# Retention attention and a SoLU MLP on one core: the whole run's written order planned anew, with q, k and v loaded by steps of their own

## The chip, the cores and the metric

The kernel runs on one core of one Trainium2 chip. The time is the device time in microseconds of one execution; lower is better. TensorE (PE), VectorE (DVE), ScalarE (ACT) and GpSimd (POOL) compute, and SyncE (SP) issues nearly all DMA transfers. All engines run their own instructions in order and wait for one another by semaphores.

## The reference

The inputs are q, k and v of 8 batches x 8 heads x 576 positions x 64, w_in (512x1024), w_out (1024x512) and g_ln (1024), all f32. The output is 4608x512 f32.

```python
# attention, for each batch and head
scores = q @ k.T / sqrt(64)
gamma  = 1 - 2.0 ** (-5 - head)
D[i,j] = gamma ** (i - j) if i >= j else 0
x      = (scores * D) @ v            # then heads side by side: 4608 x 512

# MLP
h    = x @ w_in
solu = h * softmax(h)
ln   = (solu - mean(solu)) / sqrt(var(solu) + 1e-6) * g_ln
out  = ln @ w_out
```

## The kernel before

**Tiles.** The 4608 tokens are cut into 36 chunks of 128. Nine chunks serve two batches: chunks 9g+0 to 9g+7 are four chunks of each of the two batches in turn, and chunk 9g+8 holds the last 64 tokens of both. The decay matrix is split into factors of the row and of the column, which go into q and v, and a triangular mask; what earlier chunks of a batch add comes through a running state of k times v, kept per batch.

**Steps of one chunk n**, with the names that the order uses:

- `ld` (L270, L274): loads q, k and v, three DMAs of 256 KB, on SyncE's queue.
- `cq` (L290, or L279), `ck` (L243), `cv` (L279): scale q, cast k, scale v, f32 to f16. A letter behind the chunk gives the engine: a is ACT, v is DVE, g is POOL.
- `tq` (L251): TensorE transposes of q and k into PSUM, and `eq` (L243) the copy to `qkT`. For late chunks k comes by a DMA transpose instead (`kd`, L326), and q by TensorE (`tr`, copied by `er`), or, for chunk 34, by a DMA as well (`kq`, L331).
- `sc` (L381): the scores; `mk` (L394, DVE): the mask.
- `kv` (L405), `ad` (L418, L420), `dk` (L432), `d3` (L444): this chunk's k times v, added to the state and scaled by the decay.
- `av` (L456) and `fs` (L256): scores times v, and q times the state; `ex` copies the sum to `xT`.
- `m1`, or `mr` a quarter at a time (h, L256): x times w_in into PSUM, 16 matmuls of 128x512.
- `mx` (L512), `xp` (L518), `so` (L527), `ce` (L538, L543, chunks 0 to 4 alone), `sq` (L553, L555), `ra` (L566 to L572), `rp` (L581): maximum, exponential, product, and the moments for the norm.
- `tu` and `eu`: TensorE transposes of u and the copy to `uT`; or `du` (L594): a DMA transpose of u on SyncE's queue.
- `m2` (o, L256): uT times w_out, 16 matmuls; `st` (L615, L621): scale rows on ACT, store on SyncE's queue.

The last chunk, 35, goes in halves (`hm` to `hw`). `li` and `wi` load and cast w_in in four pieces of rows; `lo` and `wo` (L789, L797) load w_out in four pieces and scale its rows by g_ln. `mm`, `mc` and `ws` (L821) take its column means away, for the chunks from 5 on. `wu` runs warm-up matmuls on zeros.

**Order.** One string, `ORDER`, lists all steps of the whole run. They are issued in just that order under a manual schedule, so each engine, and SyncE's queue too, has its steps in this order and stands still at a step whose data isn't there yet. `BANKS` gives the PSUM bank of each allocation, and `SLOTS` the slot in the SBUF ring of each tile, in the order in which they are allocated. A load waits on SyncE until its slot is free, and what stands behind it on that queue waits with it; a `du` or `kd` waits likewise for the u or k that it turns. h has two slots of two banks each.

Of the kernel before, what the change touches and what calls it, by code (L numbers as in the profile page):

```python
# [13 lines left out]
P = 128  # L14
# [15 lines left out]
tq:4 so:1 kv:4 ad:4 eq:4:a ce:1 sc:4 mk:4 cq:3:g ck:3:g tq:3 cv:3:g ld:5 xp:0 m1:2 eq:3:a so:0  # L30
kv:3 av:4 fs:4 cq:5:g lo:0 sq:1 tu:1 ex:4:a ck:5:g tq:5 eq:5:a ad:3 sc:3 ra:1:g dk:3 eu:1:a mx:2
xp:2 ce:0 m1:4 ld:6 mk:3 lo:3 mx:4 tu:0 eu:0:a sc:5 cv:5:g dk:1 cq:6:g ck:6:g wu:1:2 av:3 fs:3
xp:4 ex:3:a lo:2 kv:5 mk:5 av:5 wo:0:a fs:5 ex:5:a so:2 cv:6:g ce:2 d3:4 wo:1:g tq:6 kv:6 ad:6
lo:1 so:4 m1:3 d3:3 eq:6:a tu:2 wo:5:a ad:5 eu:2:a sc:6 wo:7:g m1:5 ld:8 rp:1 ce:4 wo:6:v mx:3
wo:3:a tu:4 eu:4:v wo:4:g wo:2:a m2:0 ld:7 sq:0 ra:0:g rp:0 m2:1 mk:6 mx:5 av:6 cq:7:v xp:3 so:3
sq:4 ra:4:v ld:9 mm:0 mc:0:v ws:6:v ws:4:v sq:2 ce:3 d3:5 ck:8:v dk:4 fs:6 ws:5:v st:1 ra:2:v
ck:7:g ws:0:v tq:7 st:0 m2:2 ex:6:a eq:7:a xp:5 cq:8:g tq:8 eq:8:a sc:7 rp:4 mk:7 m1:6 tu:3 ld:10
rp:2 st:2 ld:12 ld:11 ws:2:g sc:8 m2:4 sq:3 ws:1:v so:5 ld:13 eu:3:a dk:5 cv:7:v sq:5 mk:8 st:4
mx:6 av:7 ra:3:g rp:3 ws:7:v ck:9:a ck:10:v dk:6 fs:7 ex:7:a xp:6 m2:3 st:3 tu:5 cv:8:v kv:7 ad:7
cq:9:g so:6 tr:9 ws:3:v m1:7 dk:7 av:8 fs:8 ra:5:v rp:5 cq:10:g eu:5:a sq:6 ra:6:g er:9:va rp:6  # L40
ex:8:v mx:7 m2:5 st:5 sc:9 tu:6 eu:6:a mk:9 xp:7 so:7 ld:14 cv:9:g m1:8 av:9 kv:9 ex:9:a ck:12:a
ad:9 tr:10 mx:8 cq:12:g m2:6 cq:11:g tu:7 eu:7:v er:10:a sc:10 mk:10 ld:18 st:6 m1:9 cv:11:g sq:7
ra:7:v dk:9 cv:10:g kv:10 ad:10 ck:11:g dk:10 tr:11 xp:8 so:8 cq:13:g tr:12 av:10 rp:7 er:11:a
ex:10:a sq:8 er:12:v mx:9 m2:7 ld:15 tu:8 cq:18:g ld:17 sc:11 mk:11 eu:8:a ra:8:v cv:12:g xp:9
so:9 st:7 m1:10 rp:8 kv:11 ck:14:a av:11 d3:9 cv:13:g d3:10 fs:11 ex:11:a m2:8 ad:11 sc:12 mx:10
cq:14:g ck:13:a kv:12 ad:12 d3:12 m1:11 tu:9 ld:16 sq:9 ra:9:g st:8 tr:14 mk:12 mx:11 dk:11 xp:10
ld:19 er:14:v eu:9:a av:12 fs:12 so:10 cq:15:g cv:14:g ld:21 ex:12:a tr:13 er:13:a ck:15:a m2:9
ld:20 cq:17:v xp:11 sc:13 mk:13 tu:10 rp:9 st:9 so:11 m1:12 av:13 dk:12 fs:13 cq:16:v sc:14 mk:14
eu:10:a m2:10 sq:10 ex:13:a sq:11 kv:14 ad:14 ck:17:a mx:12 ra:11:v tu:11 cv:18:g eu:11:v cv:15:g
av:14 fs:14 ra:10:g rp:10 st:10 kv:13 m1:13 ex:14:a xp:12 d3:11 ad:13 tr:15 mx:13 so:12 du:12  # L50
ck:18:a er:15:a m2:11 xp:13 ld:22 sc:15 rp:11 st:11 dk:14 cv:16:g ck:16:g tr:16 d3:14 m1:14 d3:13
kv:15 ck:19:g mk:15 er:16:a sq:12 sc:16 av:15 dk:13 fs:15 ra:12:g so:13 ad:15 rp:12 mk:16 ex:15:a
mx:14 dk:15 cq:19:v tu:13 eu:13:a tr:17 er:17:av kv:16 xp:14 m1:15 av:16 fs:16 cq:21:g ad:16 dk:16
m2:13 sq:13 so:14 du:14 mx:15 ra:13:g rp:13 ex:16:a sc:17 mk:17 sq:14 st:13 m2:12 cv:22:v cv:17:g
av:17 fs:17 ld:23 ck:21:g tr:18 xp:15 ra:14:g so:15 ex:17:a er:18:av ld:24 m1:16 mx:16 sc:18 rp:14
ck:22:a st:12 sq:15 tu:15 mk:18 eu:15:a cq:22:g xp:16 ck:20:v ra:15:v rp:15 so:16 du:16 m2:14
tr:19 av:18 tr:21 ld:27 er:21:v st:14 m1:17 kv:18 ad:18 ex:18:a mx:17 cq:20:g tr:20 er:19:a sc:19
mk:19 er:20:a ld:25 cv:19:g m2:15 kv:19 ad:19 xp:17 cv:20:g so:17 d3:18 sq:16 ra:16:v cv:24:g
st:15 m1:18 dk:19 mx:18 av:19 sc:20 mk:20 ck:24:a rp:16 m2:16 ex:19:a cv:21:v dk:18 tu:17 kv:20
# [12 lines left out]
mk:28 st:20 m2:23 sq:24 ra:24:g tr:29 er:29:a av:27 m1:26 ra:23:v rp:23 ex:27:a rp:24 av:28 kd:31
mx:25 tr:30 xp:25 cq:31:g ex:28:a mx:26 ld:33 cv:30:g m2:22 so:25 du:25 st:23 sc:29 er:30:a mk:29
cq:32:g ck:32:g kd:32 tu:24 m1:27 xp:26 so:26 sc:30 mx:27 dk:27 st:22 kv:30 cv:31:g eu:24:a tr:32
ad:30 sq:25 d3:29 ra:25:g cv:32:g er:32:a dk:30 m1:28 kv:31 mk:30 ad:31 d3:31 xp:27 av:29 tr:31
# [4 lines left out]
so:29 du:29 m1:31 rp:27 cv:33:g kv:33 ad:33 st:27 mx:31 sq:30 m2:26 sc:34 cv:34:g mk:34 dk:33  # L80
dk:32 st:25 av:33 fs:33 xp:31 so:31 du:31 ra:28:v rp:28 ex:33:a m1:32 sq:29 av:34 kv:34 ad:34
fs:34 ex:34:a m1:33 mx:32 xp:32 m2:28 du:30 ck:35:g mx:33 xp:33 so:32 st:28 cq:35:g tr:35 er:35:v
ra:29:v rp:29 m2:29 ra:30:g so:33 sc:35 du:32 cv:35:g m1:34 du:33 mk:35 mx:34 sq:31 sq:33 dk:34
st:29 xp:34 ra:31:v rp:31 m2:31 st:31 rp:30 av:35 fs:35 rp:26 ex:35:v sq:32 so:34 du:34 m2:30
ra:32:g rp:32 ra:33:v hm:35:0 hx:35:0 st:26 st:30 hm:35:1 sq:34 hx:35:1 hp:35:0 m2:32 m2:33
ho:35:0 ht:35:0 hp:35:1 ho:35:1 hc:35 rp:33 ra:34:v ht:35:1 st:32 he:35:0:v hq:35:0:v rp:34 m2:34
he:35:1:v hq:35:1:a ra:35:v st:33 st:34 rp:35 h2:35:0 h2:35:1 hw:35:0:a hw:35:1:v
"""

BANKS = """  # L90
01231023102130121301320132013213022130232013120130212013201323013201320132013203103123001230213201
32012310231023103210320130123102130213012301032103202312030321321032103021321032113021320132132012
031132012302302102120201231232132321230123023
# [7 lines left out]
qf 012345601234561023456012345610235462  # L101
kf 012345012345021345012453012540312540
vf 012345601234561025346102350413620453
q16 012340123401234021032014321032410243
v16 012341023410234012431230124013240312
k16 012345120345120341520345124301523401
qkT 012301230123012302130210231021023103
ret0 012301230123012301230123012301230123
ret1 012301230123012301230123012301230123
t 01230120321032013201320321031210  # L110
xT 012301230123012301230123012301230210
# [754 lines left out]
```

## Time and profile before

| what | value |
|---|---|
| three runs | 211.17, 212.69, 213.72 us (median 212.69) |
| span of the profiled execution | 210.9 us; no other time of its own is recorded |
| TensorE clock | 1.00 in every stretch |
| DMA transposes | 16 of u, 7 of k, 1 of q |
| HBM read and written | 32.5 MB, 9.4 MB |

The span runs from the first to the last instruction of one execution, so it is a little less than the time of a run. Busy times are sums over the instructions of an engine. In a line that groups instructions, the figures behind the bar are the busy us, the mean ns of one, and the idle time just before them with what ended it. The DMA share is the mean over 16 DMA engines and can read a little over 1.

### The profile page before, as it was taken

To read this page: it belongs to the slowest core of one execution; us is meant where nothing else is said; L and a number is where in the kernel's file an instruction comes from. 1 tells how busy PE (TensorE), PEld (TensorE's weight loads), DVE (VectorE), ACT (ScalarE), POOL (GpSimd) and SP (SyncE) were. 2 spreads that over 40 slices of the span, in tenths; PEclk is the share of its full clock that TensorE was granted. 3 is DMA by queue.
4 is the path that set the end of the run, shared out by engine and by line. 5 is a ranking of instruction groups with operands and counts; after the bars stand their busy time and mean duration, and the time that the engine had idled before them with its cause. 6 is when DMAs were issued, how large, how long until landed. Compare 5 with 4: busy or idle time off the path is not lost.

```text
span 210.9 us, 7583 instructions
## 1 busy us (share of the span) xinstructions
PE 194.3 (92%) x3125; PEld 124.0 (59%) x3125; DVE 181.4 (86%) x323; ACT 170.5 (81%) x299; POOL 157.2 (75%) x226
## 2 busy tenths in 40 slices
PE   0887798999999999999999999999999998999992
PEld 0464476575666657657566667575656654565562
DVE  0486999979997999899989999999879998999760
ACT  2424999898979999999898978999679976677981
POOL 5377899676689899888839798879999977545620
PEclk9999999999999999999999999999999999999999
DMA  5999998999898989999999899999989999899754
GB/s 134 257 330 294 258 272 290 253 209 299 224 215 258 265 215 273 221 251 230 208 275 197 205 231 238 273 226 206 179 143 256 210 166 205 156 247 199 154 174 149
DMA packets 110834, 47.71 MB, mean 226 GB/s; under 512 B 94536, under 2 KB 104784, under 8 KB 110800
## 3 DMA queue, kind: packets, MB, share of 16 engines
q1 hardware_dynamic: 110480, 47.07, 99.7%
q8 instruction: 24, 0.39, 0.8%
q10 hardware_dynamic: 320, 0.16, 0.3%
q14 instruction: 10, 0.08, 0.2%
HBM read 32.54 MB, written 9.44 MB: 199 GB/s over the span
## 4 chain that ended last, share of the span: by engine, by line
PE 55%; SPq 14%; DMA 8%; DVE 8%; POOL 7%; ACT 3%; issue 3%; DVEq 0%; POOLq 0%
PE o L256 21%; PE h L256 18%; SPq L274 5%; SPq L270 5%; DMA w_out<-in_moe_w_out_dram 3%; PE tp L251 3%; PE sc L381 3%; PE lp L251 3%; DMA qkT<-k 2%; PE x L456 2%; POOL v L279 2%; SPq L789 2%; DMA qf<-in_q_dram 2%; PE x L256 2%; SPq L779 2%
## 5 line engine op out<-in xcount | busy, mean ns | idle before, releaser
L256 PE MATMUL h<-w_in,xT 128*64 128x512 f16 x560 | 66.9, 380 | 0.1
L256 PE MATMUL o<-w_c,uT 128*64 128x512 f16 x480 | 56.9, 380 | 0.0
L394 DVE TENSOR_TENSOR ret<-sc,tris 128x512 f16<-128x512 f32 x72 | 46.1, 682 | 2.8 <-PE sc L381 2.5
L256 PEld LDWEIGHTS <-xT 128*64 128x64 f16 x576 | 31.5, 110 | 23.1 <-issue 0.7
L512 DVE TENSOR_REDUCE nm<-h 128x1 f32<-128x1024 f32 x35 | 42.6, 1216 | 2.8 <-PE h L256 2.7
L256 PEld LDWEIGHTS <-uT 128*64 128x64 f16 x560 | 31.0, 110 | 23.0 <-issue 0.6
L527 DVE SCALAR_TENSOR_TENSOR u<-h,e 128x1024 f16<-128x1024 f32 x35 | 42.5, 1215 | 1.5 <-ACT e L518 1.4
L518 ACT ACTIVATE e<-h,nm 128x1024 f32<-128x1024 f32 x35 | 39.4, 1125 | 5.0 <-DVE nm L512 3.1
L432 POOL TENSOR_TENSOR s<-t,small 128x512 f16<-128x512 f32 x32 | 33.9, 1063 | 7.4 <-DVE t L420 6.1
L555 ACT ACTIVATE sq<-u,su 128x1024 bf16<-128x1024 f16 x30 | 34.8, 1159 | 2.0 <-DVE u L527 2.0
L581 POOL TENSOR_TENSOR rs<-w,mhalf 128x1 f32<-128x1 f32 x36 | 20.3, 570 | 20.7 <-DVE w L572 17.2
L290 POOL TENSOR_TENSOR q<-qf,small 128x512 f16<-128x512 f32 x30 | 31.2, 1043 | 5.4 <-DMA qf<-in_q_dram 5.1
L279 POOL TENSOR_TENSOR v<-vf,small 128x512 f16<-128x512 f32 x30 | 31.7, 1062 | 2.8 <-DMA vf<-in_v_dram 2.5
L615 ACT ACTIVATE o_sb<-o,rs 128x512 f32<-128x512 f32 x35 | 24.0, 692 | 4.5 <-POOL rs L581 3.2
L243 ACT COPY qkT<-tp 128x512 f16<-128x512 f16 x42 | 23.0, 599 | 5.0 <-PE tp L251 4.9
L243 ACT CAST xT<-x 128x512 f16<-128x512 f32 x29 | 17.1, 593 | 3.1 <-PE x L256 2.8
L251 PE MATMUL tp<-ident,q 128*64 128x128 f16 x232 | 12.4, 230 | 6.0 <-POOL q L290 5.5
L243 ACT CAST k<-kf 128x512 f16<-128x512 f32 x17 | 10.5, 626 | 7.7 <-DMA kf<-in_k_dram 7.7
L456 PE MATMUL x<-ret,v 128*64 128x128 f16 x288 | 14.8, 222 | 2.1 <-DVE ret L394 1.5
L251 PEld LDWEIGHTS <-q 128*64 128x64 f16 x280 | 11.0, 115 | 8.9 <-POOL q L290 5.7
L381 PE MATMUL sc<-qkT 64*128 64x128 f16 x288 | 14.7, 223 | 1.3 <-DMA qkT<-k 0.8
L444 POOL TENSOR_TENSOR s<-t,small 128x256 f32<-128x256 f32 x24 | 15.3, 638 | 0.9 <-DVE t L420 0.8
(87 smaller groups left out, 272.1 us busy)
## 6 DMA issues: line engine op xcount, KB each, us to landing
qf<-in_q_dram SPq DMA_DIRECT2D x36, 256.0 KB, 5.1
kf<-in_k_dram SPq DMA_DIRECT2D x36, 256.0 KB, 5.0
vf<-in_v_dram SPq DMA_DIRECT2D x36, 256.0 KB, 5.5
out_dram<-o_sb SPq DMA_DIRECT2D x35, 256.0 KB, 4.2
w_in<-in_moe_w_in_dram SPq DMA_DIRECT2D x4, 512.0 KB, 6.0
w_out<-in_moe_w_out_dram SPq DMA_DIRECT2D x4, 512.0 KB, 6.5
uT<-u SPq DMA_TRANSPOSE x16, 4.6
out_dram<-o_sbh SPq DMA_DIRECT2D x2, 64.0 KB, 1.8
```

The costliest lines, as they stand in the source:

```text
L243: (engine.copy if engine is nc.scalar else engine.tensor_copy)(out=out, in_=in_)
L251: nc.tensor.transpose(out=out[w], in_=in_[:, w], identity=ident)
L256: nc.tensor.matmul(out=out[w], lhsT=lhsT[:, w], rhs=rhs, start=start, stop=stop, skip_group_check=True,)
L279: engine.tensor_tensor(out=dst, in0=T.pop((key, n)), in1=table.unsqueeze(2).to_broadcast([P, H, D]), op=ALU.mult,)
L290: ENG[e].tensor_tensor(out=dst.rearrange("p (a h) d -> p h a d", h=2), in0=T.pop(("qf", n)).rearrange("p (h a) d -> p h a d", h=2), in1=ta ...
L394: nc.vector.tensor_tensor(out=r, in0=s, in1=m, op=ALU.mult)
L432: nc.gpsimd.tensor_tensor(out=s16, in0=t.unsqueeze(2).to_broadcast([P, 4, 2, D]), in1=gd.unsqueeze(3).to_broadcast([P, 4, 2, D]), op=ALU.mult,
L512: nc.vector.tensor_reduce(out=nm, in_=T["h", n], axis=AX.X, op=ALU.max, negate=True)
L518: nc.scalar.activation(out=e, in_=T["h", n], func=ACT.Exp, bias=T.pop(("nm", n)), accum_out=s)
L527: nc.vector.scalar_tensor_tensor(out=u, in0=T.pop(("h", n)), scalar=-1.0, in1=T.pop(("e", n)), op0=ALU.mult, op1=ALU.mult, accum_out=su,)
L555: nc.scalar.activation(out=s, in_=T.pop(("v", n)), func=ACT.Square, scale=-float(DFF), bias=T.pop(("su", n)), accum_out=ss,)
L615: nc.scalar.activation(out=o_sb, in_=T.pop(("o", n)), func=ACT.Copy, scale=T.pop(("rs", n)))
```

## The change

`ORDER`, `BANKS` and `SLOTS` are replaced as a whole. `ld` becomes three steps, `lq`, `lk` and `lv`, which issue the same DMAs and can be placed one by one; the first chunks' loads now have w_in's pieces between them. Which chunk uses `tq` and which `kd` with `tr` is said by the order alone. The number of rings and slots is as before.

```diff
-BY_DMA = 12
-BY_PE = (12, 13, 14, 15, 16, 18, 19, 20, 21, 22, 23, 24, 25, 27)
 ORDER = """
-c1:0 ld:1 ld:0 cq:1:g cv:1:v ck:1:a cq:0:g tq:1 eq:1:av wu:2:2 wu:5:2 ck:0:a cv:0:g sc:1 ld:2 mk:1
-tq:0 eq:0:av ck:2:a kv:0 ad:0 av:1 sc:0 mk:0 li:2 cq:2:g tq:2 ex:1:a li:3 eq:2:v dk:0 wi:3:1:a
...
-er:31:a ck:33:g so:27 du:27 fs:29 ex:29:a av:30 fs:30 ex:30:a ld:34 m2:24 tu:26 rp:25 mx:28 kd:33
-sc:31 eu:26:v sq:27 xp:28 cq:33:g mk:31 so:28 ra:27:v m1:30 mx:30 dk:31 tr:33 er:33:a st:24 m2:25
-dk:29 kv:32 sq:28 d3:30 ad:32 sc:32 m1:29 av:31 mk:32 xp:30 cq:34:g av:32 fs:32 ex:32:a so:30
-ck:34:g sq:26 fs:31 kd:34 kq:34 ex:31:v mx:29 du:28 m2:27 sc:33 ra:26:v ld:35 mk:33 d3:32 xp:29
...
+lv:1 lk:1 lv:0 lq:1 ck:1:v c1:0 cv:1:v cq:1:g li:0 cv:0:v lk:0 wu:2:4 tq:1 lq:2 kv:1 gt:0 ck:0:g
+wu:3:1 eq:1:av sc:1 wi:0:0:v mk:1 wu:6:4 kv:0 lq:0 cq:2:v li:3 c2:0 wi:3:1:v li:1 av:1 wu:8:3
...
+m1:30 du:27 lq:34 ra:25:g ad:31 ex:29:a dk:31 sc:31 so:28 ck:33:g st:24 mk:31 m2:25 sq:27 sq:26
+tr:33 d3:30 sc:32 d3:31 lq:35 mx:30 er:33:v m1:29 dk:30 kv:32 kd:33 mk:32 rp:25 xp:30 ra:26:g
+lv:33 rp:26 av:31 st:25 cv:33:g ad:32 fs:31 mx:29 m2:27 lk:35 sc:33 cq:34:g so:30 ex:31:a mk:33
+sq:28 av:32 xp:29 fs:32 kd:34 m1:31 sq:30 du:26 kq:34 so:29 av:33 ex:32:a du:29 fs:33 lv:34 kv:33
+ra:30:g du:28 mx:31 sq:29 xp:31 m1:32 cq:35:g lv:35 ex:33:v ck:35:v m2:26 ad:33 ra:27:g so:31
...
-    def ld(n):
-
-        for key, src in (("qf", q), ("kf", k), ("vf", v)):
-            dst = ring(load, [P, H, D], FP, key)
-            if key == "qf" and quads(n) or key == "kf" and chunks[n][1] == 4:
-                nc.sync.dma_start(
-                    out=dst.rearrange("p (h a) d -> p h (a d)", h=2), in_=fours(src, n)
-                )
-            else:
-                nc.sync.dma_start(out=dst, in_=tokens(src, n))
-            T[key, n] = dst
+    def load_one(n, key, src):
+        dst = ring(load, [P, H, D], FP, key)
+        if key == "qf" and quads(n) or key == "kf" and chunks[n][1] == 4:
+            nc.sync.dma_start(
+                out=dst.rearrange("p (h a) d -> p h (a d)", h=2), in_=fours(src, n)
+            )
+        else:
+            nc.sync.dma_start(out=dst, in_=tokens(src, n))
+        T[key, n] = dst
+
+    def lq(n):
+        load_one(n, "qf", q)
+
+    def lk(n):
+        load_one(n, "kf", k)
+
+    def lv(n):
+        load_one(n, "vf", v)
...
+    def both(n):
+
+        if ("qkT", n) not in T:
+            T["qkT", n] = ring(att, [P, 2, 4, P], F16, "qkT")
+        return T["qkT", n]
+
     def kd(n):
-        if chunks[n][1] == 4 or n < BY_DMA or n in BY_PE:
-            return
-        T["qkT", n] = ring(att, [P, 2, 4, P], F16, "qkT")
+
         nc.sync.dma_start_transpose(
-            out=T["qkT", n][:, 1], in_=T["k16", n].rearrange("p h d -> p (h d)")
+            out=both(n)[:, 1], in_=T["k16", n].rearrange("p h d -> p (h d)")
         )
...
     def tr(n):
-        if chunks[n][1] == 4 or n < BY_DMA or n in BY_PE:
-            return tq(n)
+
         tp = bank([P, 4, P], F16, "tr")
```

SyncE's queue, in the order written: before, the loads of chunk 1, 0 and 2, the four pieces of w_in, the loads of 4, 3 and 5, and then w_out's pieces around the loads of 6. After:

```
lv:1 lk:1 lv:0 lq:1 li:0 lk:0 lq:2 lq:0 li:3 li:1 lk:2 li:2 lv:2 lq:4 lk:4 lv:4 lk:3 lq:3 lv:3
lq:5 lk:5 lq:6 lv:5 lk:6 lo:2 lv:6 lo:1 lo:3 lo:0 lk:7 lq:7 lk:8 lq:8 lv:7 ...
```

Steps of each kind by engine, where the number changes (a is ACT, v DVE, g POOL):

| step | before | after |
|---|---|---|
| `cq` | g 31, v 5 | g 27, v 9 |
| `cv` | g 30, v 6 | g 28, v 8 |
| `ck` | a 17, g 15, v 4 | a 9, g 20, v 7 |
| `eu` | a 13, v 6 | a 15, v 3 |
| `ws` | g 1, v 7 | g 5, v 3 |
| `wi` | a 3, v 3, g 2 | a 2, v 3, g 3 |
| `ra` | g 19, v 17 | g 21, v 15 |
| `ex` | a 29, v 7 | a 30, v 6 |
| transposes of u: `du`, `tu` | 16, 19 | 17 (26 added), 18 |
| transposes of k by DMA: `kd` | 7 | 6 (29 left out) |
| warm-ups `wu`, pairs of matmuls | 10 | 15 |

More of the change, by code (lines that the diff above doesn't have):

```diff
@@ L30 @@
[L30 to L35, printed above, removed]
@@ new lines @@
+ws:1:g dk:6 lq:13 sc:7 so:5 mk:7 eq:8:a rp:4 lk:12 ws:5:g m1:6 kv:7 lk:11 lq:12 ws:7:v cq:9:v
+st:1 lq:14 cv:8:g lk:14 sc:8 ad:7 m2:4 ws:4:g lv:10 lk:13 tu:3 dk:7 lv:14 ck:9:a lv:13 mk:8 sq:5
+tu:5 lv:11 mx:6 eu:3:v sq:3 ra:5:g av:7 lk:21 st:4 xp:6 fs:7 ra:3:v tq:9 eq:9:va ex:7:a m2:3 sc:9
+cv:9:v so:6 rp:3 mk:9 m1:7 ws:3:v lv:12 eu:5:a kv:9 st:3 cq:11:g sq:6 ck:10:v ad:9 av:8 lv:15
+fs:8 rp:5 tu:6 mx:7 ck:11:g cq:10:g ra:6:g ex:8:a cv:10:g m2:5 lv:16 cq:12:g tq:10 rp:6 xp:7
+cq:14:g av:9 cq:13:v so:7 m1:8 lq:15 st:5 lk:16 ex:9:v tq:11 mx:8 eq:10:a sc:10 eu:6:a eq:11:a
@@ new lines @@
+du:14 dk:15 rp:13 rp:12 m2:13 ex:16:a lv:20 kv:18 ck:19:g xp:15 tq:17 cq:21:g m2:12 ad:18
+eq:17:va lk:25 sq:14 so:15 lk:24 dk:16 ra:14:v st:13 st:12 sc:17 sq:15 mk:17 m1:16 d3:18 sc:18
+av:17 mx:16 mk:18 xp:16 fs:17 rp:14 m2:14 ex:17:v tu:15 st:14 cq:19:g dk:18 tq:19 eu:15:a so:16
+av:18 kv:19 ra:15:v m1:17 eq:19:v tq:21 ad:19 ex:18:a ck:24:g rp:15 du:16 mx:17 lk:22 sq:16 lk:23
+sc:19 d3:19 cq:25:g mk:19 lv:22 m2:15 tq:20 xp:17 so:17 cv:20:g cq:23:g ra:16:g st:15 av:19
+eq:21:a dk:19 m1:18 cq:22:g kv:20 eq:20:v lv:21 lq:29 lv:24 ad:20 tu:17 ex:19:a mx:18 sc:20 sq:17
@@ new lines @@
+mx:33 d3:32 m2:29 av:34 so:32 fs:34 eq:35:a kv:34 st:27 ad:34 xp:33 ra:28:v ex:34:a m2:28 dk:33
+sq:32 so:33 sc:35 cv:35:g mk:35 m1:34 dk:34 du:31 st:29 rp:28 mx:34 av:35 fs:35 ra:32:g ex:35:v
+rp:30 m2:30 du:32 sq:33 ra:33:v xp:34 du:33 so:34 du:34 st:30 hm:35:0 hx:35:0 hm:35:1 rp:31
+hx:35:1 m2:31 st:28 m2:32 hp:35:1 rp:32 ho:35:1 hp:35:0 ho:35:0 ht:35:1 sq:34 m2:33 st:32 ht:35:0
+hc:35 hq:35:0:v hq:35:1:a he:35:1:v st:31 ra:34:v rp:33 rp:34 ra:35:g m2:34 rp:35 st:33 st:34
+he:35:0:v h2:35:0 hw:35:0:a h2:35:1 hw:35:1:v
@@ L88 @@
 """
 BANKS = """
[L91 to L93 removed]
+0123013013012301230231022310302130202130213201231230320132013102103213210321201320130210231023123013
+2033120123012230132032130213021032032103210321032031203103020213021031202301230203120231230123023012
+0320201320320132132132132023123120130102
@@ L100 @@
 SLOTS = """
[L101 to L107, printed above, removed]
+vf 012345601234560213650426135042613542
+kf 012345012345012340152403215432150342
+qf 012345601234560132460132460314250341
+k16 012345012435021435021430241502314250
+v16 012340123401234013240124302134213042
+q16 012340213042130241032013024032134021
+h 010101010101010101010101010101010101
+qkT 012301230123102310231023012301320312
 ret0 012301230123012301230123012301230123
 ret1 012301230123012301230123012301230123
-t 01230120321032013201320321031210
-xT 012301230123012301230123012301230210
-s16 01230132013201321032013021031201
-s32 012301230123013203120312
-h 010101010101010101010101010101010101
+t 01230123012301321023102313023103
+xT 012301230123012301230123012301230123
+s32 0123012031203102310231023
+s16 012302130213021302130213023013203
 e 01201201201201201201201201201201201
-u 01234013240132401324013241023412031
-uT 01234102341023410324102340123041230
+u 01234012340123401324013240123402103
+uT 01234210342130421034210341203412034
 o_sb 01230123012301230123012301230123012
@@ L331, in kq @@
         nc.sync.dma_start_transpose(
-            out=T["qkT", n][:, 0], in_=T.pop(("q16", n)).rearrange("p h d -> p (h d)")
+            out=both(n)[:, 0], in_=T.pop(("q16", n)).rearrange("p h d -> p (h d)")
         )
     def tr(n):
-        if chunks[n][1] == 4 or n < BY_DMA or n in BY_PE:
-            return tq(n)
         tp = bank([P, 4, P], F16, "tr")
@@ L344, in er @@
     def er(n, e="a"):
-        if chunks[n][1] == 4 or n < BY_DMA or n in BY_PE:
-            return eq(n, e)
-        turned(ENG[e], n, T["qkT", n][:, 0], T.pop(("tp", n)))
+        turned(ENG[e], n, both(n)[:, 0], T.pop(("tp", n)))
     def turned(engine, n, out, tp):
```

94 lines of the change are left out of this document (43 added, 51 removed).

## Prediction

> **What bounds the kernel now.** I read the share of each engine first, then the same shares in stretches of the run, then TensorE's waits in the long middle, and last the chain that ended last.
>
> ```profile
> span 210.9 us, 7583 instructions
> PE 194.3 (92%) x3125; PEld 124.0 (59%) x3125; DVE 181.4 (86%) x323; ACT 170.5 (81%) x299; POOL 157.2 (75%) x226
> PE 55%; SPq 14%; DMA 8%; DVE 8%; POOL 7%; ACT 3%; issue 3%; DVEq 0%; POOLq 0%
> ```
>
> TensorE is busy for 92% of the span and is more than half of the chain. VectorE follows at 86%. SyncE's queue and the transfers, 22% of the chain together, must lie somewhere in particular, which the stretches show (columns: stretch, its length, then busy us and count for PE, weight loads, DVE, ACT and POOL, then TensorE's clock, the DMA share and GB/s).
>
> ```profile
> 20.00:25.00 5.00, 3.48 (x60) 2.29 (x59) 4.24 (x7) 3.70 (x7) 4.36 (x6) 1.00 1.00 236
> 30.00:40.00 10.00, 9.32 (x175) 6.38 (x171) 9.79 (x18) 8.80 (x15) 9.61 (x12) 1.00 1.01 274
> 40.00:200.00 160.00, 157.20 (x2548) 99.51 (x2547) 148.44 (x257) 140.77 (x247) 125.54 (x176) 1.00 1.04 222
> 205.00:211.00 6.00, 2.08 (x36) 1.71 (x32) 0.66 (x2) 1.39 (x3) 0.55 (x1) 1.00 0.37 131
> ```
>
> There are three stages. Until 40 us the transfers are full and TensorE has gaps. From 40 to 200 us TensorE has 157.20 of 160 us, so 2.8 us are left to win there; DVE has 148.44, and the clock is full. The last 6 us are the tail of the last chunk, whose steps the change keeps. The chain says what the first stage waits for, and with what TensorE is filled later (start, us, what):
>
> ```profile
> 31.84 7.28 DMA w_out<-in_moe_w_out_dram
> 39.13 1.33 ACT w_out L797 x2
> ...
> 173.57 5.15 DMA qkT<-k
> ...
> 178.76 0.40 PE sc L381 x8
> ...
> 185.70 0.12 PE kp L405 x8
> 185.83 0.23 PE x L256 x8
> 186.05 1.73 PE h L256 x16
> 187.78 1.73 PE o L256 x16
> 189.51 0.45 PE tp L251 x16
> ```
>
> The first stage ends when the last piece of w_out has landed at 39.12 us and has been scaled at 40.46. Later the chain is matmul after matmul without a gap, except at 173.57, where the DMA transpose of k of chunk 33 holds the scores. TensorE's waits from 40 to 200 us (what waited, for what: total, times, longest):
>
> ```profile
> PE sc L381 <- DMA qkT<-k: 0.8, 1, 0.8
> PE x L456 <- POOL v L279: 0.5, 1, 0.5
> PE tp L251 <- DVE t L420: 0.5, 1, 0.5
> PE tp L251 <- DVE k L243: 0.4, 1, 0.4
> PE o L256 <- ACT w_out L797: 0.3, 1, 0.3
> PE tr L251 <- ACT o_sb L615: 0.3, 1, 0.3
> ```
>
> Six single waits make up the 2.8 us. No one of them recurs, so the written order before fits the chip almost everywhere.
>
> **The change, part by part.** No matmul for the result is added or removed. An h or o step costs the same 1.73 us at another place. u of chunk 26 leaves TensorE for a DMA transpose and k of chunk 29 comes to it, 0.45 and about 0.2 us, which I leave out as near zero. What can move the time is: the first 40 us, which engine does the small copies, and how much TensorE work stands between the issue of a transfer and its use.
>
> *The start.* The loads are now ordered one by one, and pieces of w_in go between them. But w_out's last piece stands in the SyncE queue behind 21 loads of 256 KB, four pieces of w_in and the three other pieces of w_out, before as after. With the DMA share at 1.00 to 1.01 the same bytes take the same time, and w_out lands at 39.1 us again. Ahead of the first step that needs w_out, TensorE has 23.8 us of written work before and 24.8 after, summed by the chain's prices; the difference is five more warm-ups of two 128x512 matmuls each, 5 x 2 x 1.73/16 = 1.1 us, and both sums lie well under 39 us. The warm-ups lie in gaps such as that between 20 and 25 us (3.48 busy of 5); without these they would cost 1.1. I take 0, from -0.3 (half of the 0.7 us in which TensorE is idle from 30 to 40 us) to +0.5 (half of the warm-ups).
>
> *Which engine copies.* By the written orders: q's scaling on DVE 5 to 9 (POOL 31 to 27), v's on DVE 6 to 8 (POOL 30 to 28), k's cast from ACT 17 to 9, on DVE 4 to 7, on POOL 15 to 20; uT's eviction on DVE 6 to 3, on ACT 13 to 15; centring of w_out on DVE 7 to 3, on POOL 1 to 5.
>
> ```profile
> L290 DVE TENSOR_TENSOR q<-qf,small 128x512 f16<-128x512 f32 x5 | 4.9, 982 | 1.1 <-DMA qf<-in_q_dram 1.1
> L290 POOL TENSOR_TENSOR q<-qf,small 128x512 f16<-128x512 f32 x30 | 31.2, 1043 | 5.4 <-DMA qf<-in_q_dram 5.1 <-POOL v L279 0.2
> L279 DVE TENSOR_TENSOR v<-vf,small 128x512 f16<-128x512 f32 x6 | 4.1, 690 | 6.1 <-DMA vf<-in_v_dram 6.1
> L279 POOL TENSOR_TENSOR v<-vf,small 128x512 f16<-128x512 f32 x30 | 31.7, 1062 | 2.8 <-DMA vf<-in_v_dram 2.5
> L243 ACT CAST k<-kf 128x512 f16<-128x512 f32 x17 | 10.5, 626 | 7.7 <-DMA kf<-in_k_dram 7.7
> L243 POOL CAST k<-kf 128x512 f16<-128x512 f32 x15 | 9.1, 609 | 0.9 <-DMA kf<-in_k_dram 0.7
> L243 DVE CAST k<-kf 128x512 f16<-128x512 f32 x4 | 1.8, 443 | 0.0
> L243 ACT COPY uT<-lp 128x1024 f16<-128x1024 f16 x13 | 13.3, 1022 | 0.5 <-PE lp L251 0.4
> L243 DVE COPY uT<-lp 128x1024 f16<-128x1024 f16 x6 | 4.1, 685 | 0.6 <-PE lp L251 0.5
> L821 DVE TENSOR_TENSOR w_c<-w_out,warm 128x512 f16<-128x512 f16 x7 | 3.4, 500 | 0.0
> L821 POOL TENSOR_TENSOR w_c<-w_out,warm 128x512 f16<-128x512 f16 x1 | 1.1, 1149 | 0.0
> ```
>
> DVE: 4 x 0.98 + 2 x 0.69 + 3 x 0.44 - 3 x 0.69 - 4 x 0.50 = +2.6 us. ACT: -8 x 0.63 + 2 x 1.02 = -3.0. POOL: -4 x 1.04 - 2 x 1.06 + 5 x 0.61 + 4 x 1.15 = +1.4. (Some smaller steps also change engine, one or two of a kind; they are left out.) DVE comes to 151 of 160 us in the middle stage, still under TensorE's 157.2, which covers it; without cover it would be +2.6. I take +0.3, since the nearer a second engine comes to the first the more often one waits for the other; bounds 0 to 2.6.
>
> *Waits of before.* A new order removes those 2.8 us where they were and may put as many elsewhere. It gives k of chunk 29 to TensorE instead of a DMA transpose, and ACT, at 140.77, 3.0 us of air. I take half, -1.4; bounds -2.8 to 0.
>
> TensorE's own figure may hide waits: in the trace its busy time counts modelled ends, and 157.20 is made of matmuls that overlap. The Trainium skill, "Perfetto Trace Analysis", section "Identifying the Most-Contended Engine", says that matmul busy time is not a good measure, since pipelined instructions look different from what they cost. By it more than 2.8 us may be there to win, and the term -1.4 would grow by half of what is hidden. The gapless chain at 185 us (0.12, 0.23, then 1.73 twice) bears the small figure out for that stretch only.
>
> *Transposes and loads at new places.* This is the largest part. Between the place where a transfer is written and its first use stands TensorE work, which I add up with the chain's prices (h or o 1.73 us, scores 0.3 to 0.4, x, fs and kv 0.1 to 0.2, transposes of a chunk 0.45). For the DMA transposes of u, from `du` to `m2`, this cover was 5.7 us at least before and 8.7 in the median; after, it is 2.4 for chunk 26, 3.3 for 23, 3.5 for 32, 4.1 for 31, 4.9 for 22, 5.0 for 27, 6.4 in the median. For k, from `kd` to `sc`, it was 8.9 for chunk 33 and 5.7 for 34; after, 2.2 for 33, 4.0 for 32, 5.1 for 30. The times from issue to landing, of uT and then of qkT:
>
> ```profile
> DMA to landing us min/median/max: 3.4/4.6/5.7
> ...
> DMA to landing us min/median/max: 2.5/3.1/5.1
> ```
>
> At the medians, issued just at their written place, they come late by 2.2 (26), 1.3 (23), 1.1 (32), 0.5 (31) and 0.9 (k of 33) = 6.0 us. At the longest it is 3.3 + 2.4 + 2.2 + 1.6 + 0.8 + 0.7 + 0.3 + 0.2 for u and 2.9 + 1.1 for k = 15.5. At best nothing: SyncE's queue goes in its own order and can be ahead of the written place (u of 26 is ready some 16 us of TensorE work before its `du`). It can also be behind: before, k of 33 was issued at 173.57, and its scores waited although 8.9 us of work stood between. What is late next is the o matmul or the scores, and behind them on TensorE everything, since it works in order. I take half of 6.0, +3.0; bounds 0 to 15.5.
>
> The loads' cover for v falls from 16.8 to 7.8 us in the median, for k and q it stays (10.0 to 9.4, 10.3 to 12.5).
>
> ```profile
> vf<-in_v_dram SPq DMA_DIRECT2D x36, 256.0 KB, 5.5
> ```
>
> Only v of chunk 33 is written with next to nothing, 0.2 us, before its scaling; that one holds POOL by 5.3 us, which has 34 of 160 us free, and 4.9 us more of TensorE work stand before `kv` needs it: 5.5 + 1.06 - 0.2 - 4.9 = 1.5 at full price. Queued behind it on POOL are q of 34 and a row scale. I take +0.4; bounds 0 to 1.5.
>
> **Sum.** 0 + 0.3 - 1.4 + 3.0 + 0.4 = +2.3. On the profile's span: 210.9 + 2.3 = 213.2. The runs' median lies 1.8 above the span, so 212.69 + 2.3 = 215.0.
>
> **Rivals.** *No change, 212.7:* the queue runs ahead wherever the cover is short, and the old waits come again at other places. For it speaks that the two u transposes with 5.7 us, the longest landing exactly, cost nothing before; against it that k of 33 was late with more.
> *Faster, 209.9:* transposes hidden as in the first rival, ACT's relief and the freely placed loads take away the waits of the middle stage, 212.69 - 2.8. It would decide if no transfer is waited for by TensorE. For it speaks that each q, k and v load can now stand where it is wanted, as POOL's 5.1 us of waits for q show; against it that TensorE's own waits from 40 us on hold none for a load, so that loads in better places have nothing of TensorE's to give back.
> *Late at full price, about 220:* SyncE's queue is held at its head by a slot or an unfinished u, as at 173.57, and all five late transposes cost in full: 212.69 + 6.0 + 0.3 + 0.4 to 1.5 = 219.4 to 220.5, with no old wait removed. It decides from the point where SyncE has no lead in the last third of the run.
>
> **How the numbers follow.** The forecast, transposes late at about half price, 213.5 to 217.5, has 0.40; no change 0.24; faster 0.26; full price 0.10. About 1%, 2.1 us, is what a measurement of this kernel can tell. Of the forecast a quarter, 0.10, lies under 214.8. So: faster 0.26, same 0.24 + 0.10 = 0.34, slower 0.30 + 0.10 = 0.40. The range goes from 209.5 (the faster rival with the best start, 212.69 - 2.8 - 0.3 = 209.6) to 219.5, which leaves out most of the full price and what might be won beyond the 2.8.
>
> **What would show it.** Right: in the changed profile TensorE waits in `o` for the transfer of uT and in `sc` for that of qkT, 2 to 4 us together, mostly after 130 us; the last piece of w_out lands at 39 to 39.5 us; TensorE's busy time is equal within 1.5 us, DVE's is up by some 2, ACT's down by 3. Wrong: w_out lands two us earlier or later (the start moves the time after all), or TensorE waits for no transfer in the middle stage (then the first two rivals), or it waits for POOL or DVE instead, which my sum puts at 0.7 in all.

## The result and the profile after

The changed kernel takes 220.88 us (median of 4 runs, 220.62 to 221.36), beside 213.2 us for the kernel before on the same chip. The ratio is 1.041 (95% interval 1.036 to 1.046): slower by 4%, some 8 us. Ratios, here and below, compare runs in the faster of the chip's two states alone, so they need not be the quotient of the two medians. The forecast was 215.0 us, and the range ended at 219.5.

The page of the changed kernel, for the same three lines as before:

```profile
span 219.1 us, 7596 instructions
PE 197.1 (90%) x3127; PEld 123.9 (57%) x3127; DVE 188.0 (86%) x321; ACT 167.7 (77%) x293; POOL 163.3 (75%) x234
PE 39%; DVE 33%; ACT 10%; DMA 7%; SPq 5%; issue 4%; POOL 0%; DVEq 0%
```

VectorE's share of the chain has gone from 8% to 33%, and TensorE's from 55% to 39%. VectorE is busy for 188.0 us instead of 181.4. The stretches of the changed kernel (columns as before: stretch, its length, then busy us and count for PE, weight loads, DVE, ACT and POOL, then clock, DMA share and GB/s):

```profile
0.00:40.00 40.00, 28.17 (x467) 17.67 (x469) 30.05 (x54) 23.24 (x40) 28.27 (x43) 1.00 1.02 267
40.00:200.00 160.00, 153.63 (x2477) 97.00 (x2474) 148.49 (x247) 133.00 (x231) 130.18 (x179) 1.00 0.98 213
200.00:220.00 20.00, 15.30 (x192) 9.19 (x186) 9.44 (x23) 11.42 (x24) 4.90 (x13) 0.95 0.63 156
```

In the middle stage TensorE is busy for 153.6 us where it was 157.2, and makes 71 matmuls less in the same 160 us. No one place holds the loss. Summed over TensorE's instructions, the same amount of work is 1.6 us late at 40 us, 3.1 at 62, 4.9 at 94, 7.0 at 137 and 8.4 at the end. So it is lost a piece at a time, up to about 140 us above all. TensorE's longest waits from 40 us on:

```profile
PE o L259 <- DMA uT<-u: 1.5, 2, 1.1
PE tp L254 <- DVE q L300: 1.3, 1, 1.3
PE sc L392 <- DMA qkT<-k: 0.6, 1, 0.6
PE sc L392 <- ACT qkT L246: 0.5, 2, 0.3
PE kp L416 <- DVE ret L405: 0.4, 1, 0.4
```

The transposes are in the list (2.1 us, against 0.8 before), as the prediction said, but they are a small part of 8. The last row teaches something: `kv` needs v and k, not the masked scores `ret`. What it waits for is the PSUM bank of the scores, which VectorE hasn't read out yet: `kv` of chunk 7 has the bank that the scores of chunk 7 had, and starts at 52.64 us, 0.05 us after the mask has read it. The waits of the other engines, over the whole run, show what is late behind this:

```profile
ACT e L529 <- DVE nm L523: 13.4, 15, 1.9
...
DVE qkT L246 <- ACT qkT L246: 5.5, 4, 2.9
...
ACT qkT L246 <- DVE qkT L246: 3.8, 4, 1.9
```

Idle time of these engines is not yet time lost by the kernel: of the 5.5 us, 2.9 lie at 10 us, where VectorE had to wait for most of that time for the transposes themselves. In the kernel before, the two kinds of wait between `qkT` and `qkT` have one row together:

```profile
DVE qkT L243 <- ACT qkT L243: 0.3, 1, 0.3
```

The eviction of a chunk's q and k, `eq`, copies two halves of one PSUM bank. Its letters say which engine copies which: `a` or `v` is one engine for both, `av` or `va` is a half each. The new order has twelve such splits, the old one six. One of the steps at which a split holds TensorE is that of chunk 17 of the changed kernel:

```profile
108.42 0.68 DVE L246 COPY qkT<-tp 128x512 f16<-128x512 f16 x1
109.14 0.58 ACT L246 COPY qkT<-tp 128x512 f16<-128x512 f16 x1 [0.62 <-DVE qkT L246]
109.78 0.40 PE L392 MATMUL sc<-qkT 64*128 64x128 f16 x8 [0.26 <-ACT qkT L246]
```

ScalarE's half begins 0.04 us after VectorE's has ended (108.42 + 0.68 = 109.10); ScalarE stood still for 0.62 us before it, with its next steps queued behind, and the scores come after both. In none of the eighteen splits of the two traces do the halves overlap, and in all of them the half written first runs first. The old kernel's chunk 17 shows why its splits cost it little: the second engine had other work until long after the first half was done. So it was in three of the six (0.3 to 1.2 us between the halves); in the other three the second engine stood still for 0.06 to 0.29 us only.

```profile
98.10 0.61 ACT L243 COPY qkT<-tp 128x512 f16<-128x512 f16 x1
...
99.84 0.68 DVE L243 COPY qkT<-tp 128x512 f16<-128x512 f16 x1
```

The Trainium skill, "PSUM — Partial Sum Buffer", section "PSUM bank collisions raise a hardware error", says that two engines may not access the same bank and partitions at once, reads against reads included, and that a dependency is put between them. The trace agrees (0.03 us at the least between the halves). The shared destination tile alone doesn't make this wait: in the kernel before, ScalarE and VectorE cast two halves of one piece of w_in, from one SBUF tile into one other, at the same time. ScalarE's is the last of its three casts in this row, from 17.30 to 17.92 us.

```profile
16.02 1.90 ACT L243 CAST w_in<-w_in 128x512 f16<-128x512 f32 x3 [2.57 <-DMA w_in<-in_moe_w_in_dram]
...
17.54 0.75 DVE L243 CAST w_in<-w_in 128x512 f16<-128x512 f32 x1
```

What the halves of `eq` share and these don't is the PSUM bank. No run put the two halves of `eq` into two banks, so that this would end the wait is not shown.

### The profile page after: what moved, and what is told of

Its sections match the earlier page's. It is cut to its first block, busy times and chain, and to the rows that moved or that the text cites. A ratio compares the mean times of both kernels' runs of the same rounds, so it can differ in the third digit from the quotient of the medians.

```text
span 219.1 us, 7596 instructions
## 1 busy us (share of the span) xinstructions
PE 197.1 (90%) x3127; PEld 123.9 (57%) x3127; DVE 188.0 (86%) x321; ACT 167.7 (77%) x293; POOL 163.3 (75%) x234
## 4 chain that ended last, share of the span: by engine, by line
PE 39%; DVE 33%; ACT 10%; DMA 7%; SPq 5%; issue 4%; POOL 0%; DVEq 0%
PE o L259 16%; PE h L259 11%; DVE ret L405 7%; DVE nm L523 6%; DVE u L538 6%; DMA vf<-in_v_dram 3%; ACT qkT L246 3%; PE sc L392 3%; DVE v L289 2%; DMA uT<-u 2%; PE tp L254 2%; DMA qkT<-k 2%; DVE t L431 2%; DVE u L554 2%; SPq L790 2%
## 5 line engine op out<-in xcount | busy, mean ns | idle before, releaser
L259 PEld LDWEIGHTS <-uT 128*64 128x64 f16 x560 | 31.8, 110 | 25.2 <-DMA uT<-u 2.1
L246 ACT COPY qkT<-tp 128x512 f16<-128x512 f16 x44 | 24.1, 596 | 16.6 <-PE tp L254 12.8
L289 POOL TENSOR_TENSOR v<-vf,small 128x512 f16<-128x512 f32 x28 | 29.8, 1064 | 7.7 <-DMA vf<-in_v_dram 7.4
L300 POOL TENSOR_TENSOR q<-qf,small 128x512 f16<-128x512 f32 x26 | 28.7, 1106 | 4.8 <-DMA qf<-in_q_dram 4.7
L592 POOL TENSOR_TENSOR rs<-w,mhalf 128x1 f32<-128x1 f32 x36 | 21.0, 588 | 5.5 <-DVE w L583 5.1
L246 ACT CAST xT<-x 128x512 f16<-128x512 f32 x30 | 17.8, 594 | 4.8 <-PE x L467 3.4
L392 PE MATMUL sc<-qkT 64*128 64x128 f16 x288 | 15.3, 218 | 2.8 <-ACT qkT L246 1.3
L246 POOL CAST k<-kf 128x512 f16<-128x512 f32 x20 | 12.9, 644 | 5.6 <-DMA kf<-in_k_dram 5.4
L392 PEld LDWEIGHTS <-qkT 64*128 64x128 f16 x288 | 8.5, 94 | 13.5 <-issue 6.4
```

The source lines that it names most:

```text
L246: (engine.copy if engine is nc.scalar else engine.tensor_copy)(out=out, in_=in_)
L259: nc.tensor.matmul(out=out[w], lhsT=lhsT[:, w], rhs=rhs, start=start, stop=stop, skip_group_check=True,)
L289: engine.tensor_tensor(out=dst, in0=T.pop((key, n)), in1=table.unsqueeze(2).to_broadcast([P, H, D]), op=ALU.mult,)
L300: ENG[e].tensor_tensor(out=dst.rearrange("p (a h) d -> p h a d", h=2), in0=T.pop(("qf", n)).rearrange("p (h a) d -> p h a d", h=2), in1=ta ...
L392: nc.tensor.matmul(out=s[e][:, hp], lhsT=qkT[dd, 1, hp], rhs=qkT[dd, 0, hp], start=True, stop=True,)
```

## The experiments

Ratios are to the kernel before, run beside each on the same chip. The medians of that kernel in these comparisons lie between 212.0 and 213.8 us, so a difference of 1 us between medians of different rows says little by itself. Three theories stood at the start: D, VectorE's added copies; T, the prediction's late transposes and loads; O, the sequence as such. X, the splits, and K, the choice of banks, came from the later traces.

| kernel | what differs | median us | ratio (95% interval) |
|---|---|---|---|
| changed | | 220.88 | 1.041 (1.036 to 1.046) |
| a_k_act | changed, 6 casts of k off VectorE | 219.84 | 1.030 (1.024 to 1.036) |
| a_qv_pool | changed, 13 scalings off VectorE | 218.80 | 1.025 (1.017 to 1.033) |
| a_dve | both | 219.11 | 1.032 (1.028 to 1.035) |
| a_dve_xfer | a_dve, four transposes earlier | 221.97 | 1.049 (1.040 to 1.057) |
| a_nosplit | changed, no split evictions | 216.10 | 1.014 (1.005 to 1.022) |
| a_nosplit_qv | a_nosplit with a_qv_pool | 216.95 | 1.018 (1.008 to 1.027) |
| a_nosplit_xfer | a_nosplit, three transposes earlier | 217.68 | 1.023 (1.017 to 1.028) |
| a_banks | changed, banks by measured times | 222.01 | 1.043 (1.032 to 1.055) |
| a_shares | changed order, old engines | 232.05 | 1.087 (1.081 to 1.094) |
| b_shares | old order, new engines | 255.61 | 1.197 (1.188 to 1.206) |
| b_split | before, with the new splits | 217.15 | 1.018 (1.010 to 1.026) |
| b_nosplit | before, no splits | 212.81 | 0.999 (0.995 to 1.004) |
| b_banks | before, other banks | 220.57 | 1.039 (1.035 to 1.043) |
| ba_start, ab_start | orders spliced at chunk 0's o | 226.61, 219.98 | 1.066, 1.034 |
| ba_half, ab_half | orders spliced at chunk 16's h | 221.87, 232.06 | 1.046, 1.091 |
| ba_start2 | ba_start, banks by measured times | 223.11 | 1.051 (1.045 to 1.057) |

### Engines exchanged between the orders

```diff
# a_shares: each of 104 letters of the changed order as in the order before, such as
-cv:9:v ... ck:12:g ... eq:13:va
+cv:9:g ... ck:12:a ... eq:13:a
# b_shares: the other way round
```

> The changed kernel's order, with each small step (scalings, casts, evictions, row scales, centring) on the engine that it has in the kernel before. Theory D (VectorE is full in long stretches of the first 150 us, because more SBUF-only copies are on it and each of these takes up to twice as long beside GpSimd): at least half of the 7.7 us comes back, 214 to 217 us, VectorE's busy time falls from 188 to about 182. Theory T (the prediction's: late DMA transposes and loads): within 1 us of 220.9, since no transfer moves. Theory O (the sequence itself, whatever the engines): 219 us or more, and the new engines may even cost, since the order was made for the old ones.

> The kernel before with its own order and loads, but each small step on the engine that it has in the changed kernel (chunk 29's k still goes by a DMA transpose). Theory D: 3 to 6 us slower than before, 216 to 219 us, with VectorE's busy time near 187. Theory T: within 1 us of before. Theory O: slower too, since the order was made for other engines, but with VectorE no fuller than 183.

Both are far slower, 232 and 256 us, and none of the theories named such a size; 232 lies in theory O's range for a_shares, which was open at its upper end (219 or more). VectorE's busy time moved about as theory D expected in both (184.7 and 188.2 us), so the amount of work on it doesn't explain the loss. What they show is that an order and its engines belong together: a step's place in the list is right for the engine it was placed for. b_shares also shows a wait that the kernel before doesn't have, TensorE for the state from GpSimd:

```profile
PE x L255 <- POOL s L431: 5.7, 1, 5.7
```

As a test of D they are inconclusive, and smaller edits were needed.

### Work taken off VectorE

```diff
# a_k_act: chunks 4, 10, 14, 20, 21, 35
-ck:4:v
+ck:4:a
# a_qv_pool: q of 5, 8, 9, 13, 24, 27, 32; v of 9, 11, 12, 16, 21, 22
-cq:5:v ... cv:9:v
+cq:5:g ... cv:9:g
# a_dve: both
```

> The changed kernel with six casts of k (chunks 4, 10, 14, 20, 21, 35) moved from VectorE to ScalarE, the rest as it is. Theory D: VectorE loses about 4 us of work, ScalarE takes 3.8 us at 0.63 each; 1 to 3 us faster than the changed kernel, 218 to 220. Theory T: no change within 0.5 us. Theory O: no change or slower.

> The changed kernel with thirteen scalings of q (chunks 5, 8, 9, 13, 24, 27, 32) and v (9, 11, 12, 16, 21, 22) moved from VectorE to GpSimd. Theory D: VectorE loses 11 to 12 us, GpSimd gains 13.7 at 1.05 each (163 to 177 us); 2 to 5 us faster, 216 to 219, unless GpSimd becomes the next bound, which would show as TensorE waits for q and v from GpSimd. Theory T: no change within 0.5 us. Theory O: no change or slower.

> The changed kernel with both moves off VectorE at once: six casts of k to ScalarE and thirteen scalings of q and v to GpSimd. Theory D, as the single moves left it (1.0 and 2.1 us): 217 to 218.5 us if they add, and not nearer than 216 to before, so that most of the loss has another cause. Theory O (the sequence): 218 to 220.

By the medians a_k_act gives back 1.0 us and a_qv_pool 2.1, each at the low end of what D expected; by the ratios it is 2.3 and 3.4, and a_k_act's interval touches that of the changed kernel. Together they don't add: a_dve stands at 219.1, where theory O had it, with VectorE at 174.7 us, 7 below the kernel before. So VectorE's load is a part of it, some 2 us (1.8 by a_dve's median, 2.0 by its ratio), and cannot be the main cause.

### Transposes written earlier

```diff
# a_dve_xfer: SyncE's order
-... du:20 ... du:23 ... du:22 ... st:20 kd:30 ... er:33:v ... kd:33 ... du:27 ... du:26
+... du:20 du:22 ... ck:30:a kd:30 ... er:33:v kd:33 ... du:27 du:26
# and SBUF slots of qkT, s32, s16 and uT in that order
```

> a_dve with the DMA transposes that TensorE waited for in the changed kernel written earlier on SyncE's queue, where their data is ready: u of 22 right behind u of 20, u of 26 behind u of 27, k of 30 behind its cast, k of 33 behind the copy of q of 33. Theory T: 2 to 4 us faster than a_dve. Theory D or O: 0.5 to 1.5 us faster, since TensorE's waits for these transposes are 2.2 us in the profile and some of it comes back elsewhere.

It became 2.9 us slower than a_dve, which no theory had. TensorE's waits in this kernel between 140 and 160 us, and ScalarE's:

```profile
PE tr L252 <- ACT xT L244: 2.4, 1, 2.4
...
ACT k L244 <- DMA kf<-in_k_dram: 3.9, 1, 3.9
```

u of 22 went ahead of the loads that stood between its old and its new place; the two transposes of u now hold SyncE's queue from 143.92 us on:

```profile
143.92 4.91 SPq L603 DMA_TRANSPOSE uT<-u  x2
```

A load of k behind them came late, ScalarE stood at its cast, the eviction of xT behind that kept its bank, and TensorE waited for the bank. So a transpose moved to where its data is ready takes its place from something else. The same without u of 22, on the best of the changed kernels:

```diff
# a_nosplit_xfer
-... st:20 kd:30 ... er:33:v ... kd:33 ... du:27 ... du:26
+... ck:30:a kd:30 ... er:33:v kd:33 ... du:27 du:26
# and SBUF slots of qkT, s32 and s16
```

> a_nosplit with three DMA transposes written earlier where no load has to stand behind them longer: u of 26 behind u of 27, k of 30 behind its cast, k of 33 behind the copy of q of 33. TensorE waits 1.4 us for the first two in a_nosplit. Theory T: 1 to 2 us faster than a_nosplit, 214 to 215. If the queue gives the time back elsewhere, as in a_dve_xfer: within 1 us of 216.1 or slower.

217.68 us against 216.10. In its profile 1.1 us of the lag are there by 40 us already, where the two are written alike, so the difference may be smaller than it looks; but nothing came back. TensorE's rows show 0.9 us of waits for transposes in a_nosplit, less than the 1.4 expected, and 0.8 are left, for one of k. So theory T falls for the transposes: the waits for them are real, and writing them earlier gained nothing. The loads at new places were not moved in a run of their own.

### Orders spliced

```diff
# ba_start, ba_half: the order before up to m2:0 or m1:16, then what is left in the changed order
# ab_start, ab_half: the other way round
# SBUF slots and PSUM banks of all four: the longest free by the written order
```

> The kernel before's order up to its first o matmul (chunk 0), then the changed kernel's order for all that is left, each step on the engine that its part's order gives; SBUF slots and PSUM banks by the longest free. Theory S (the start loses the time, and the rest only carries it): near 213 to 215 us. Theory P (the loss is made piece by piece, at tight places all through the order; the lag of TensorE's work is 1.6 us at 40 us and 8.4 at the end): 218 to 220. Theory T (late transposes and loads alone, all after 130 us): as P here, 219 to 221.

> The changed kernel's order up to its first o matmul, then the order before for the rest. Theory S: 218 us or more. Theory P: 214 to 216. Theory T: within 1 us of before.

> The order before up to the h matmuls of chunk 16 (about 105 us), then the changed order. By the lags in the two profiles (5.1 of 8.4 us at that point), theory P gives +3.3 us: 215.5 to 217.5. Theory S: 213 to 214. Theory T: 219 to 221.

> The changed order up to the h matmuls of chunk 16, then the order before. Theory P: +5.1 us, 217 to 219.5. Theory S: 218 or more. Theory T: within 1 us of before.

ba_start and ba_half came out slower than any theory had it. ab_start and ab_half lie in theory S's range, which was open at its upper end (218 or more), but ba_start, 226.6 us where S had 213 to 215, speaks against S. A reason lies in the splicing: the first half of ba_half has the order, the engines and the loads of before, and yet TensorE's work was 6.6 us late at 105 us. Only banks and a few slots differ there. So the cut says nothing on where the order loses time, and the banks had to be tried alone:

```diff
# b_banks: the kernel before; order, engines and slots as they are
 BANKS = """
-01231023102130121301320132013213022130...
+01230120312130213202310320130321032320...
```

> The kernel before with one string changed: the PSUM bank of each allocation is now the one whose last reader stands first in the written order; order, engines, loads and SBUF slots as before. It is the rule by which banks were given in the four spliced kernels. If that rule is what made ba_half's first half late (6 to 7 us at chunk 16, with the order before), this is 4 to 8 us slower than before, 217 to 221 us, and the spliced kernels say little of the order. If it is harmless, within 1 us of before.

220.57 us: with not one step moved, this costs as much as the whole change (1.039 against 1.041). The waits that it makes are of the same kind as `kp` on `ret` above. Two of TensorE's in b_banks:

```profile
PE o L255 <- DVE ret L393: 1.5, 1, 1.5
...
PE sc L380 <- DVE uT L242: 0.7, 1, 0.7
```

The o matmul needs uT and w_out, and the scores need qkT. Four banks serve all of TensorE's small results, and one taken in the wrong turn stops it until VectorE or ScalarE comes to read it.

> As ba_start (the order before up to the first o matmul, then the changed order), but with the banks of before up to the cut and then the bank whose last reader ended first by the measured times of the changed kernel. If the bank rule spoiled the spliced kernels: 219 to 221 us, with the start's 1.6 us back and the rest of the loss as in the changed kernel. Otherwise 226 as ba_start.

With better banks the spliced kernel is 3.5 us faster than ba_start, but not at the 219 to 221 us that a clean splice would have had; what it says of the start stays open.

### Banks of the changed kernel

```diff
# a_banks: for each allocation the bank whose last reader ended first in the changed kernel's trace;
# and a few SBUF slots of s32 and s16
```

> The changed kernel with the PSUM bank of each allocation chosen anew: the one whose last reader ended first by the changed kernel's own measured times; order and engines as they are. Theory K (the wait for a PSUM bank is the largest part of the loss, 4.6 us after 40 us against 1.6 before, and comes from a bad choice of banks): 2 to 3 us faster, 218 to 219. If the banks are as well chosen as they can be and are only read late: within 1 us.

No change (1.043). In the changed kernel's trace some 20 steps of TensorE from 40 us on begin just as their bank comes free, about 5 us of idle time, against 5 steps and 1.6 us before. In seven of them the copy that frees the bank also makes what the step needs (the o of 3, 6 and 10, the scores of 9, the x of 6, 15 and 16), so not all of it is the bank's. And its banks are already as good as that rule makes them: this choice gains nothing, and another was not tried. Theory K falls as far as this rule goes, and the question becomes why the readers are late.

### Split evictions

```diff
# a_nosplit: twelve chunks, six to each engine
-eq:7:av eq:9:va eq:12:va eq:13:va ...
+eq:7:v eq:9:a eq:12:v eq:13:a ...
# b_split: the kernel before, chunks 7, 12, 13, 14, 15, 23, 27 split as in the changed order; 0 and 17 with halves exchanged
-eq:7:a ... er:12:v ... er:13:a
+eq:7:av ... er:12:va ... er:13:va
```

> The changed kernel with each of its twelve q/k evictions that are split between ScalarE and VectorE (before: six) given whole to one engine, six to each, so that both keep their work. Theory X (the halves run one after the other, each engine standing still for the other's: 9.3 us of such waits in the changed profile, 0.3 before): 1.5 to 4 us faster than the changed kernel, 217 to 219.5, and those waits gone. Theory O (only the tight sequence): within 1 us of it or slower.

> The kernel before with the changed kernel's splits of the q/k evictions (thirteen split where six were), three halves more on VectorE. Theory X: 1 to 4 us slower than before, 214 to 217, with waits of one half's engine for the other's. Otherwise within 1 us.

This is the main cause. With as many halves on each engine as in the changed kernel, twelve tokens give back 4.8 us by the medians (5.8 by the ratios), and the ratio goes from 1.041 to 1.014, intervals apart. The time comes back where the splits stand: from 62 to 137 us, with six of them, the changed kernel falls from 3.1 to 7.0 us behind, a_nosplit from about 2 to about 3. The rows of waits between `qkT` and `qkT` are gone from a_nosplit's list, and TensorE is nearly as busy in the middle stage as before the change, 156.5 us:

```profile
40.00:200.00 160.00, 156.54 (x2538) 98.66 (x2536) 149.78 (x253) 136.68 (x238) 132.31 (x185) 1.00 1.04 218
```

In the order before, the same splits, with three halves more on VectorE, cost 1.0 to 2.6%, about 3.9 us, and the waits come up, on ScalarE and from there on TensorE's scores:

```profile
ACT qkT L242 <- DVE qkT L242: 4.9, 3, 2.2
...
PE sc L380 <- DVE qkT L242: 1.8, 2, 1.0
```

> a_nosplit with the thirteen scalings of q and v on GpSimd too. If X and D add: 215 to 217 us. If VectorE's queue is one cause behind both: 217 to 218.5.

Without splits, taking the scalings off VectorE gains nothing more (1.018 against 1.014). 216.95 us lies just inside the range for X and D adding, but that range was set before a_nosplit had given 216.1; from there, adding would have meant some 214. The 2 us of a_qv_pool seem to be the same time: a VectorE with less to do comes sooner to its half. That is argued from the sum, not shown by a run of its own.

```diff
# b_nosplit: the kernel before
-eq:1:av eq:0:av er:9:va er:17:av er:18:av er:26:av
+eq:1:v eq:0:a er:9:v er:17:a er:18:v er:26:a
```

> The kernel before with its six split evictions given whole to one engine, three to each. Its profile shows 0.3 us of waits of one half for the other, so theory X expects no change beyond 1 us; a gain of more would say that splits cost more than the waits named.

No change, as X expected. So a split is not dear by itself: six of them, placed where the second engine is busy anyway, cost nothing that can be measured. Twelve, most of them at places where it isn't, cost some 5 us. No version found is faster than the kernel before.

## Why the prediction was wrong, step by step

**What bounds the kernel.** Right that TensorE is the bound. The 2.8 us that it has to give back in the middle stage are too few, as the prediction itself allowed. In the trace the busy time of a matmul runs to its modelled end, 380 ns for one of h though 16 of them take 1.73 us, and so covers part of a pause behind it. Counted from start to start, pauses of over 0.12 us beyond that pace add up to 11 us after 40 us. The picture also left out how little room lies behind TensorE: ScalarE's waits for VectorE's maxima were in the profile of before too, and rose fourfold in the middle stage (3.1 to 12.8 us) with 3 us less work on ScalarE.

**The start.** Taken as 0, up to 0.5. TensorE was busy for 28.2 of the first 40 us (30.0 before) and was 1.6 us behind at 40. The last piece of w_out landed at 38.6 us, near the 39.1 forecast, but its last scaling, on VectorE, ended at 41.4 instead of 40.5: from 28 to 59 us the chain runs along VectorE almost without a break. So what holds the start is not the transfer alone, as the term had it. But the start itself moves by about 1 us with the same steps (1.1 between the traces of a_nosplit and a_nosplit_xfer), and a_dve, with less on VectorE, is as late at 62 us (3.3), so the size and the cause of a loss here aren't shown.

**Which engine copies.** This is the step that failed, in two ways: the forecast let TensorE's work cover VectorE's and took +0.3. First, evictions of q and k were passed over among the "smaller steps": by engine, the counts of halves hardly move (16 against 17 on VectorE). That six split evictions became twelve, with one engine standing still for the other in most, was in the diff and is the largest cost, about 5 of the 8 us. Second, VectorE's own sum was too low, +2.6 us where +6.6 were measured. The prices were those of the rows before, and most of those that count rose:

```profile
L289 DVE TENSOR_TENSOR v<-vf,small 128x512 f16<-128x512 f32 x8 | 7.9, 990 | 0.0
L246 DVE CAST k<-kf 128x512 f16<-128x512 f32 x7 | 4.8, 679 | 5.4 <-DMA kf<-in_k_dram 5.4
L554 DVE TENSOR_SCALAR u<-u,nmu 128x1024 f16<-128x1024 f16 x5 | 4.6, 912 | 0.2
L405 DVE TENSOR_TENSOR ret<-sc,tris 128x512 f16<-128x512 f32 x72 | 46.0, 679 | 3.9 <-PE sc L392 3.6
```

Scaling v took 690 ns before and 990 after, casting k 443 and 679, `ret`, which reads PSUM, 682 and 679. Scaling q went the other way, 982 and 837, with two of five long ones before and two of nine after. Only operations that read SBUF alone became longer, though not every one of them: of the eight scalings of v the five longest (0.85 to 1.51 us) ran beside GpSimd for most of their time, and the other three kept 0.67 to 0.69, one of them beside GpSimd too, as three scalings of q did (0.68 to 0.69). The Trainium skill, "GPSIMD Engine Reference", section "Specifications", says that GpSimd's SBUF interfaces are shared with VectorE, with contention for instructions with two SBUF inputs or in a two-port mode; the trace agrees in part, since some of these instructions ran beside GpSimd at their old price. The effect of the whole on the time, as far as a_k_act, a_qv_pool and a_dve show it, is 1 to 3 us instead of 0.3, and it overlaps with that of the splits. The prediction's own sign of this came: from 40 us on TensorE waits 2.8 us for VectorE (0.9 before), where its sum had 0.7 for VectorE and GpSimd together.

**Waits of before.** Taken as half removed, -1.4. They did go from their places, but others came: the pauses of over 0.12 us, counted from start to start as above, add up to 18 us after 40 us instead of 11.

**Transposes and loads at new places.** The largest term, +3.0. The waits came, at u of 22 and 26 and k of 30, two of the six u transposes and one of the three of k that were named as short, 2.1 us by TensorE's waits against 0.8. So the mechanism was there at under half its price, and it isn't where most of the time went: written earlier, the transposes gave nothing back, twice.

**Loads.** +0.4. GpSimd waited 2.2 us for v of 33, less than the 5.3 that were put down, and TensorE shows no wait for it from 40 us on. Near enough.

**Rivals.** "Late at full price, about 220" had the time and the sign by luck: its mechanism gave 1.3 us more of waits, not 6.0. No rival had two engines waiting for each other.

**What stays open.** After the splits some 1.4%, 3 us, remain, of which about 2 are there by 62 us in a_nosplit's trace. The late transposes are not it by themselves, nor is VectorE's load; what is left is the waits for banks (about 4 us in a_nosplit against 1.6, counted as above) and the start. None of them was taken away alone.

## What to carry to other kernels

When a written order changes, compare not only how many steps each engine has, but which steps make one engine wait for another: an eviction shared by two engines is faster only if both may work at the same time, and here they never did. A plan for all engines is one thing with its engine letters and its buffer turns; exchanging all letters cost 5 and 20% of the order's own time, and another turn of the banks 4% in one order and nothing in the other, so prices of single steps don't add up to its time. And where TensorE waits on something that it doesn't read, look for the bank: here the waits on `ret` were of that kind.

## What was not expected of the hardware

Two copies from one PSUM bank by two engines ran strictly one after the other, 0.03 us apart at the least, in all eighteen cases, while two casts into halves of one SBUF tile overlapped. VectorE's scalings from SBUF to SBUF ran up to 2.2 times as long beside GpSimd (1.51 us instead of 0.68), though not each of them, while its operations that read PSUM kept their time. And the turn in which four PSUM banks are used was worth 3.9% (3.5 to 4.3) with nothing else changed.
